# A decode attention block rewritten as one hand-synchronised section

## The chip, the cores and the metric

The kernel runs on one core of one Trainium2 chip. The metric is device time in microseconds, the median of several executions. A core has TensorE (PE in the profile; its weight loads are PEld), VectorE (DVE), ScalarE (ACT), GpSimd (POOL) and SyncE (SP, which here only issues DMAs), and 16 DMA engines that move data between HBM and the on-chip memory (SBUF). TensorE writes its products to a second on-chip memory, PSUM.

## The reference

One decode step of a transformer block: attention over cached keys and values, a feed-forward layer beside it, and a residual sum. All data is float32.

```python
B, Sq, D = 4, 1, 512
H, Sk, Dh = 32, 4096, 128          # k_cache, v_cache: (B, H, Sk, Dh), 268 MB each
F = 1792
xn = _layernorm(x)
q = (xn @ wq).reshape(B, Sq, H, Dh).transpose(0, 2, 1, 3)
scores = einsum("bhqd,bhkd->bhqk", q, k_cache) * Dh ** -0.5
o = einsum("bhqk,bhkd->bhqd", softmax(scores), v_cache)
a = o.transpose(0, 2, 1, 3).reshape(B, Sq, H * Dh) @ wo
f = silu(xn @ w1) @ w2
return x + a + f
```

There is one query row for each batch and head, so every key and every value is used once: 537 MB of caches are read for little arithmetic.

## The kernel before

The work is cut into T = 32 tiles. Tile i is one batch (`i % 4`) and a group of four heads (`i // 4`): 128 partitions, each with R = 128 consecutive positions of 128 numbers, 64 KB a partition, so that 32 partitions hold one head. A tile of K is 8.39 MB and so is a tile of V.

`load_tile` (L72) issues each tile as one DMA from SP. K has two buffers (`kpool`) and V one (`vpool`). The second K buffer first serves as scratch for x, w1 and the intermediate rows, the V buffer first holds wq. A scheduler (the Tile framework) puts in all waits and keeps each engine's instructions in an order of its choice. SP issues in a fixed order: K of tile i+1, then V of tile i.

- `scores` (L228): in four steps of 32 rows, VectorE multiplies K in place by the tile's query, which lies in PSUM spread over the partitions (L235). Of the 32 row sums VectorE takes 24 (`tensor_reduce`, L239); ScalarE takes 8, one `activation` with an accumulated sum each (L241).
- `queries` (L215): once per four tiles, TensorE spreads the queries into PSUM by products with columns of the identity (L221).
- `maxima` and `softmax` (L245, L252): VectorE takes each partition's maximum (L247), TensorE turns the column into a row (L249), VectorE takes the maximum of each head (L255), TensorE spreads it (L259), ScalarE forms the bias (L261) and the four exponentials with their sums (L265). The exponentials go into `p_t`, four columns a row, of which one is not zero.
- `values` (L271): 32 products of TensorE with the V tile, written out in Python for every tile, into one of two PSUM buffers (L277).
- `heads_out` (L285): TensorE sums the exponentials (L289), ScalarE copies the PSUM buffer (L291), VectorE forms the reciprocal and weights (L295, L297), TensorE collects the heads (L300), ScalarE copies them (L305).
- `project` (L307): once per four tiles, the product with a 1 MB piece of wo (`load_wo`, L82, 2 KB runs), added to `acc` in PSUM (L135).

After the last tile, w2 is loaded in four pieces into the V buffer and its products are added to `acc`; VectorE copies it (L359) and four DMAs, two from SP and two from ACT, write the result (L362).

Of the kernel before, what the change touches and what calls it, by code (L numbers as in the profile page):

```python
# [8 lines left out]
F32 = mybir.dt.float32  # L9
# [4 lines left out]
EPS = 1e-5  # L14
G = 4
STEP = 32
ACT_ROWS = 8
LAST_K_CUTS = (64,)
LAST_V_CUTS = (64, 96)
W2_CUTS = (7, 11, 13)  # L20


@with_exitstack
def kernel(
# [11 lines left out]

# [17 lines left out]
    FC = F // P  # L54
    PH = P // G
    R = S * G // P
    T = H // G * B
    NR = 4
# [8 lines left out]
    small = ctx.enter_context(tc.tile_pool(name="small", bufs=2))  # L67
    ps_q = ctx.enter_context(tc.tile_pool(name="ps_q", bufs=2, space=bass.MemoryType.PSUM))
    ps_s = ctx.enter_context(tc.tile_pool(name="ps_s", bufs=3, space=bass.MemoryType.PSUM))
    ps_1 = ctx.enter_context(tc.tile_pool(name="ps_1", bufs=1, space=bass.MemoryType.PSUM))  # L70

    def load_tile(pool, name, cache, i, cuts=()):  # L72
        t = pool.tile([P, R, Dh], F32, name=name)
        h, b = i // B * G, i % B
        src = cache[b, h : h + G].rearrange("h s d -> (h s) d")
        src = src.rearrange("(p r) d -> p r d", p=P)
        edges = (0, *cuts, R)
        for a, z in zip(edges[:-1], edges[1:]):
            nc.sync.dma_start(t[:, a:z, :], src[:, a:z, :])
        return t  # L80

    def load_wo(g):  # L82
        t = wpool.tile([P, G, D], F32, name="wo_t")
        nc.sync.dma_start(
            t, wo[g * G * Dh : (g + 1) * G * Dh, :].rearrange("(h p) n -> p h n", p=P)
        )
        return t


    scratch = kpool.tile([P, R, Dh], F32, name="k_t").rearrange("p r d -> p (r d)")  # L90
    x_sb, xc, sq, xn = (scratch[:B, n * D : (n + 1) * D] for n in range(4))
    NP = 2 * PH - B
    FJ = F // 4
    xpad = scratch[:, 4 * D : 4 * D + DC * NP].rearrange("p (c n) -> p c n", c=DC)
    h_sb = scratch[:, 5 * D : 5 * D + FJ]
    w1_t = scratch[:, 6 * D : 6 * D + DC * F].rearrange("p (c f) -> p c f", c=DC)
    nc.sync.dma_start(x_sb, xf)
    nc.sync.dma_start(w1_t, w1.rearrange("(p c) f -> p c f", p=P))
    wq_t = vpool.tile([P, R, Dh], F32, name="v_t").rearrange("p (c m) d -> p c (m d)", c=DC)
    nc.sync.dma_start(wq_t, wq.rearrange("(p c) n -> p c n", p=P))  # L100
    ks = {0: load_tile(kpool, "k_t", k_cache, 0)}

    ident = const.tile([P, P], F32, name="ident")
    make_identity(nc, ident)
    same = const.tile([P, P], F32, name="same")
    nc.gpsimd.memset(same, 0.0)
    for g in range(G):
        nc.gpsimd.memset(
            same[g * PH : (g + 1) * PH, :].rearrange("p (a g) -> p a g", g=G)[:, :, g], 1.0
        )  # L110
    one = const.tile([1, 1], F32, name="one")
    nc.gpsimd.memset(one, 1.0)
    nc.vector.memset(xpad, 0.0)
    p_t = const.tile([P, R, G], F32, name="p_t")
    nc.gpsimd.memset(p_t, 0.0)

    o_ps = []
    for n in range(2):
        t = ps_1.tile([P, NR * Dh], F32, name=f"o_ps{n}")
        nc.vector.memset(t, 0.0)  # L120
        o_ps.append(t)
    acc = ps_1.tile([P, P], F32, name="acc")
    nc.vector.memset(acc, 0.0)

    pick = const.tile([P, NR * G], F32, name="pick")
    nc.vector.tensor_reduce(
        pick,
        ident.rearrange("p (j m) -> p m j", j=4)[:, : NR * G, :],
        axis=AX, op=ALU.add,
    )  # L130

    def accumulate(lhsT, rhs, start=False, stop=False):

        for j in range(D // P):
            nc.tensor.matmul(  # L135
                acc[32 * j : 32 * j + B, :], lhsT, rhs[:, j * P : (j + 1) * P],
                start=start, stop=stop,
            )

    accumulate(ident[:B, :B], x_sb, start=True)  # L140


    nmean = const.tile([B, 1], F32, name="nmean")
    nc.vector.tensor_reduce(nmean, x_sb, axis=AX, op=ALU.add)
    nc.vector.tensor_scalar_mul(nmean, nmean, -1.0 / D)
    nc.vector.tensor_scalar_add(xc, x_sb, nmean)
    var = const.tile([B, 1], F32, name="var")
    nc.vector.tensor_mul(sq, xc, xc)
    nc.vector.tensor_reduce(var, sq, axis=AX, op=ALU.add)
    nc.vector.tensor_scalar(var, var, 1.0 / D, EPS, op0=ALU.mult, op1=ALU.add)  # L150
    rstd = const.tile([B, 1], F32, name="rstd")
    nc.scalar.activation(rstd, var, AF.Sqrt)
    nc.vector.reciprocal(rstd, rstd)

    t1 = const.tile([B, 1], F32, name="t1")
    nc.vector.tensor_mul(t1, rstd, rstd)
    nc.vector.tensor_mul(t1, t1, var)
    nc.vector.tensor_scalar(t1, t1, -0.5, 1.5, op0=ALU.mult, op1=ALU.add)
    nc.vector.tensor_mul(rstd, rstd, t1)
    nc.vector.tensor_scalar_mul(xn, xc, rstd)  # L160


    xt_ps = ps_s.tile([P, DC, B], F32, name="sm")
    xn_c = xn.rearrange("b (p c) -> b c p", c=DC)
    for c in range(DC):
        nc.tensor.transpose(xt_ps[:, c, :], xn_c[:, c, :], ident[:B, :B])
    xnT = const.tile([P, DC, B], F32, name="xnT")
    nc.vector.tensor_copy(xnT, xt_ps)
    nc.vector.tensor_copy(xpad[:, :, PH - B : PH], xt_ps)

    hp = ps_s.tile([P, FJ], F32, name="sm")
    for c in range(DC):
        for j in range(4):
            nc.tensor.matmul(
                hp[32 * j : 32 * j + B, :], xnT[:, c, :], w1_t[:, c, j * FJ : (j + 1) * FJ],
                start=(c == 0), stop=(c == DC - 1),
            )
    for j in range(4):  # L180
        rows = slice(32 * j, 32 * j + B)
        nc.scalar.activation(h_sb[rows, :], hp[rows, :], AF.Silu)
    ht_ps = ps_s.tile([P, FC, B], F32, name="sm")
    h_f = h_sb.rearrange("b (m f) -> b f m", f=FC)
    for f in range(FC):
        for j in range(4):
            rows = slice(32 * j, 32 * j + B)
            nc.tensor.matmul(
                ht_ps[32 * j : 32 * j + 32, f, :], h_f[rows, f, :], ident[rows, rows],
                start=True, stop=True,  # L190
            )
    hT = const.tile([P, FC, B], F32, name="hT")
    nc.vector.tensor_copy(hT, ht_ps)


    HJ = H // 4
    qp = ps_s.tile([P, Dh], F32, name="sm")
    for hl in range(HJ):
        for c in range(DC):
            for j in range(4):  # L200
                h = HJ * j + hl
                a = PH - B - B * hl
                nc.tensor.matmul(  # L203
                    qp[32 * j : 32 * j + 32, :],
                    xpad[:, c, a : a + PH],
                    wq_t[:, c, h * Dh : (h + 1) * Dh],
                    start=(hl == 0 and c == 0),
                    stop=(hl == HJ - 1 and c == DC - 1),
                )
    q_all = const.tile([P, Dh], F32, name="q_all")  # L210
    nc.vector.tensor_copy(q_all, qp)  # L211

    q_ps, vs, st, ls, ot_g, wo_t = {}, {}, {}, {}, {}, {}

    def queries(n):  # L215

        t = ps_q.tile([P, B, Dh], F32, name="q_ps")
        for b in range(B):
            for g in range(G):
                r = (n * G + g) * B + b  # L220
                nc.tensor.matmul(  # L221
                    t[g * PH : (g + 1) * PH, b, :],
                    ident[:, r : r + 1].to_broadcast([P, PH]), q_all,
                    start=True, stop=True,
                )
            q_ps[n * B + b] = t[:, b, :]

    def scores(i, a):  # L228

        k, q = ks[i], q_ps[i]  # L230
        if a == 0:
            st[i] = small.tile([P, R], F32, name="s")
        s = st[i]
        z = a + STEP
        nc.vector.tensor_tensor(  # L235
            k[:, a:z, :], k[:, a:z, :], q[:, None, :].to_broadcast([P, STEP, Dh]), op=ALU.mult
        )
        v = z - ACT_ROWS
        nc.vector.tensor_reduce(s[:, a:v], k[:, a:v, :], axis=AX, op=ALU.add)  # L239
        for r in range(v, z):  # L240
            nc.scalar.activation(  # L241
                k[:, r, :], k[:, r, :], AF.Copy, accum_out=s[:, r : r + 1]
            )
# [151 lines left out]
```

## Time and profile before

| | |
|---|---|
| runs (3) | 1321.89, 1322.12 and 1322.5 us; median 1322.12 |
| span of the profiled execution, first to last instruction | 1320.8 us |
| busy: VectorE, ScalarE, TensorE, GpSimd | 1008.8, 415.9, 405.6, 1.9 us |
| read from HBM | 561.00 MB, 425 GB/s over the span |

The profile shows one execution. Its span leaves out what lies before the first and after the last instruction, so a run's time is a little longer: 1.3 us at the median. In a group's row stand the line, engine and operation, the tile written and the tile read, the shapes and the count; behind the first bar the busy time in us and the mean of one in ns; behind the second the idle time in front of it and who ended it. In a row in order of time the first two numbers are start and duration in us.

### The profile page before, as it was taken

The page shows a single profiled execution, that of the slowest core. Times are in us where ns is not written, and L with a number is a line of the kernel's source. Part 1 is how long each engine was busy: PE and PEld are TensorE (multiplying, and loading weights), DVE is VectorE, ACT ScalarE, POOL GpSimd, SP SyncE. Part 2 cuts the span into 40 slices and gives each one's busy share as a digit, 9 for nine tenths or more (in the row PEclk, how much of TensorE's full clock was granted, in tenths as well). Part 3 has the DMA queues.
Part 4 walks back from the last instruction along what each step waited for, and adds up shares of the span by engine and source line. Part 5 has one row for each costly group of instructions (what it writes and reads, how often), then busy time and mean ns, then how long its engine had stood idle before and what let it go on. Part 6 is the DMA issues. An engine that isn't in the chain of part 4 may idle for free.

```text
span 1320.8 us, 10238 instructions
## 1 busy us (share of the span) xinstructions
PE 405.6 (31%) x3500; PEld 165.4 (13%) x3500; DVE 1008.8 (76%) x406; ACT 415.9 (31%) x2408; POOL 1.9 (0%) x13
## 2 busy tenths in 40 slices
PE   2312333320343312433322333221334211333207
PEld 1301111100111100111100111010111000111003
DVE  1499967987677986777977777977768977778990
ACT  1143333333333332333232333332323333323331
POOL 0000000000000000000000000000000000000000
PEclk8756666655666656666556666556666556666558
DMA  9999999999999999999999999999999999999996
GB/s 404 436 439 425 429 435 425 439 435 423 441 431 429 427 433 425 439 433 420 442 423 433 437 420 427 433 425 439 422 429 427 431 441 425 431 423 427 425 429 250
DMA packets 14827, 561.65 MB, mean 425 GB/s; under 512 B 1316, under 2 KB 1332, under 8 KB 5688
## 3 DMA queue, kind: packets, MB, share of 16 engines
q1 hardware_dynamic: 14760, 561.01, 98.9%
q8 instruction: 27, 0.44, 0.1%
q14 instruction: 24, 0.20, 0.0%
q10 hardware_dynamic: 16, 0.00, 0.0%
HBM read 561.00 MB, written 0.01 MB: 425 GB/s over the span
## 4 chain that ended last, share of the span: by engine, by line
DMA 54%; DVE 31%; PE 12%; another core or an unknown queue 1%; issue 1%; ACT 0%; SPq 0%; DVEq 0%; ACTq 0%
DMA k_t<-in_A_k_cache_dram 38%; DVE k_t L235 19%; DMA v_t<-in_A_v_cache_dram 13%; DVE s L239 12%; PE o_ps L277 9%; DMA v_t<-in_A_wq_dram 2%; PE q_ps L221 1%; PE sm L203 1%; PE acc L135 0%; ACT o_sb L291 0%; PE sm L300 0%; ACT p_t L265 0%; PE sm L249 0%; DVE m L247 0%
## 5 line engine op out<-in xcount | busy, mean ns | idle before, releaser
L235 DVE TENSOR_TENSOR k_t<-k_t,q_ps 128x4096 f32<-128x4096 f32 x128 | 559.9, 4415 | 204.9 <-DMA k_t<-in_A_k_cache_dram 204.9
L241 ACT ACTIVATE k_t<-k_t 128x128 f32<-128x128 f32 x1024 | 301.4, 295 | 636.3 <-DVE k_t L235 627.8
L277 PE MATMUL o_ps<-v_t,p_t 128*16 128x512 f32 x1984 | 280.9, 729 | 559.9 <-DMA v_t<-in_A_v_cache_dram 556.1
L239 DVE TENSOR_REDUCE s<-k_t 128x24 f32<-128x3072 f32 x128 | 422.9, 3344 | 0.0
L241 ACT ACTIVATION_READ_ACCUMULATOR k_t<-k_t 128x1 f32 x1024 | 191.2, 187 | 0.0
L277 PEld LDWEIGHTS o_ps<-v_t,p_t 128*16 128x16 f32 x1984 | 65.8, 113 | 752.8 <-issue 752.4
L265 ACT ACTIVATE p_t<-s,nb 32x128 f32<-32x128 f32 x128 | 66.0, 516 | 2.5
L221 PE MATMUL q_ps<-q_all,ident 128*32 128x128 f32 x256 | 13.8, 389 | 171.0 <-DVE k_t L235 170.6
L291 ACT ACTIVATE o_sb<-o_ps 128x512 f32<-128x512 f32 x32 | 19.1, 596 | 130.1 <-PE o_ps L277 130.1
L300 PE MATMUL sm<-w,o_sb 128*128 128x4 f32 x256 | 41.5, 285 | 21.9 <-DVE w L297 20.5
L249 PE MATMUL sm<-ident,m 128*1 128x128 f32 x32 | 9.1, 284 | 126.3 <-DVE m L247 126.3
L300 PEld LDWEIGHTS sm<-w,o_sb 128*128 128x128 f32 x256 | 39.6, 236 | 25.4 <-issue 16.9
L305 ACT ACTIVATE ot_g<-sm 128x4 f32<-128x4 f32 x32 | 5.7, 178 | 102.3 <-PE sm L300 102.3
L255 DVE TENSOR_REDUCE gm<-sm 1x4 f32<-1x128 f32 x32 | 8.9, 278 | 30.7 <-PE sm L249 30.7
L221 PEld LDWEIGHTS q_ps<-q_all,ident 128*32 128x32 f32 x256 | 10.2, 156 | 172.6 <-DVE k_t L235 171.1
L265 ACT ACTIVATION_READ_ACCUMULATOR p_t<-s,nb 32x1 f32 x128 | 25.0, 196 | 0.0
L249 PEld LDWEIGHTS sm<-ident,m 128*1 128x1 f32 x32 | 2.5, 79 | 153.8 <-DVE m L247 137.2
L211 DVE COPY q_all<-sm 128x128 f32<-128x128 f32 x1 | 0.3, 292 | 24.0 <-PE sm L203 24.0
L259 PE MATMUL sm<-gm,one 1*128 1x4 f32 x64 | 15.4, 309 | 3.3 <-DVE gm L255 3.3
L295 DVE RECIPROCAL rl<-sm 128x1 f32<-128x1 f32 x32 | 4.8, 150 | 14.5 <-PE sm L289 14.5
L203 PE MATMUL sm<-v_t,k_t 128*32 128x128 f32 x256 | 10.4, 335 | 13.7 <-DMA v_t<-in_A_wq_dram 11.3
L135 PE MATMUL acc<-wo_t,ot_g 128*4 128x128 f32 x256 | 13.6, 380 | 0.3 <-ACT ot_g L305 0.3
(55 smaller groups left out, 117.7 us busy)
## 6 DMA issues: line engine op xcount, KB each, us to landing
wo_t<-in_A_wo_dram SPq DMA_DIRECT2D x8, 1024.0 KB, 49.6
k_t<-in_A_k_cache_dram SPq DMA_DIRECT2D x2, 4096.0 KB, 37.9
k_t<-in_A_v_cache_dram SPq DMA_DIRECT2D x1, 4096.0 KB
k_t<-in_A_v_cache_dram SPq DMA_DIRECT2D x2, 2048.0 KB
k_t<-in_B_w_dram SPq DMA_DIRECT2D x1, 3584.0 KB, 11.3
v_t<-in_B_w_dram SPq DMA_DIRECT2D x1, 1792.0 KB, 13.1
v_t<-in_B_w_dram SPq DMA_DIRECT2D x1, 1024.0 KB, 15.2
v_t<-in_B_w_dram SPq DMA_DIRECT2D x1, 512.0 KB
```

Source lines behind the costliest of these rows:

```text
L135: nc.tensor.matmul(acc[32 * j : 32 * j + B, :], lhsT, rhs[:, j * P : (j + 1) * P], start=start, stop=stop,)
L203: nc.tensor.matmul(qp[32 * j : 32 * j + 32, :], xpad[:, c, a : a + PH], wq_t[:, c, h * Dh : (h + 1) * Dh], start=(hl == 0 and c == 0), sto ...
L221: nc.tensor.matmul(t[g * PH : (g + 1) * PH, b, :], ident[:, r : r + 1].to_broadcast([P, PH]), q_all, start=True, stop=True,)
L235: nc.vector.tensor_tensor(k[:, a:z, :], k[:, a:z, :], q[:, None, :].to_broadcast([P, STEP, Dh]), op=ALU.mult)
L239: nc.vector.tensor_reduce(s[:, a:v], k[:, a:v, :], axis=AX, op=ALU.add)
L241: nc.scalar.activation(k[:, r, :], k[:, r, :], AF.Copy, accum_out=s[:, r : r + 1])
L249: nc.tensor.transpose(mt, m, ident)
L259: nc.tensor.matmul(mb, one.to_broadcast([1, P]), gm, start=True, stop=True)
L265: nc.scalar.activation(p_t[rows, :, g], s[rows, :], AF.Exp, bias=nb[rows, g : g + 1], scale=scale, accum_out=l[rows, :],)
L277: nc.tensor.matmul(o[j : j + NR * G, :], p_t[:, rows, :].rearrange("p r g -> p (r g)"), v[:, rows, :].rearrange("p r d -> p (r d)"), start ...
L291: nc.scalar.activation(o_sb.rearrange("p r d -> p (r d)"), o_ps[i % 2], AF.Copy)
L300: nc.tensor.matmul(ot, o_sb[:, r, :], w[:, r, :], start=(r == 0), stop=(r == NR - 1))
```

## The change

The Tile scheduler's part is replaced by one `tile_critical` section in which every wait is written by hand. A small class, `Queue`, keeps a semaphore and a count for each engine; loads have semaphores of their own.

- Row sums: ScalarE has none left. VectorE multiplies 32 rows as before; GpSimd then adds the upper 64 of a row's 128 products to the lower 64; VectorE sums the 64 that remain (`add`), one step behind.
- Queries: `q_col` holds them as columns. `spread` makes each tile's query in PSUM by one 32 x 32 block transpose of VectorE, in the middle of the tile ahead. The factor -scale is folded into the query, so maxima become minima.
- Maxima: VectorE alone, as a minimum, a transpose and a minimum. The exponential takes the result as its bias directly, and puts its sums into one column of `sums` a tile.
- Values: a hardware loop on TensorE (`Fori`), one body for 31 tiles: wait for the weights and V, 32 products into one PSUM buffer, wait for ScalarE's copy, four collecting products into column i of `o_t`.
- Division by the sums and the product with wo happen once, after all tiles. wo is one load in two pieces (32 KB runs) into the V buffer; w2 goes into a K buffer; the last V goes into the other.
- Placement: small tiles come first, and a fill tile puts the three large buffers on multiples of 256 B. x is loaded from the ACT queue; the output leaves in two DMAs.

The core of the diff (the layer norm and the input products keep their arithmetic):

```diff
-    kpool = ctx.enter_context(tc.tile_pool(name="kpool", bufs=2))
-    vpool = ctx.enter_context(tc.tile_pool(name="vpool", bufs=1))
-    wpool = ctx.enter_context(tc.tile_pool(name="wpool", bufs=1))
+    small([P, -(CONST_AT + taken) % 256 // 4 + 64], "fill")
+    kb = [big.tile([P, R, Dh], F32, name=f"k{n}") for n in range(2)]
+    vb = big.tile([P, R, Dh], F32, name="v")
...
+        got_w1 = load(sp, "w1", w1_t, w1.rearrange("(p c) f -> p c f", p=P))
+        got_x = load(act, "x", x_sb, xf)
+        got_wq = load(sp, "wq", wq_t, wq.rearrange("(p c) n -> p c n", p=P))
+        got_k = {0: load(sp, "k0", kb[0], cache(k_cache, 0))}
...
+        got_k[1] = load(sp, "k1", kb[1], cache(k_cache, 1), p_h, d_h, p_xt)
+        def spread(i):
+            dve.wait(d_col)
+            return dve.done(
+                nc.vector.transpose(
+                    q_b[:, i % 2, :], q_col[:, i, :, None].to_broadcast([P, G, PH])
+                )
+            )
...
+        for i in range(T):
+            k, s = kb[i % 2], s_t[i % 2]
+            if i > 0:
+                if i + 1 < T:
+                    got_k[i + 1] = load(
+                        sp, f"k{(i + 1) % 2}", kb[(i + 1) % 2], cache(k_cache, i + 1),
+                        scored[i - 1],
+                    )
+            if i + 1 < T:
+                got_v[i] = load(
+                    sp, "v", vb, cache(v_cache, i), p_q if i == 0 else (values_done, i)
+                )
+            dve.wait(spread_q[i], got_k[i])
...
+            def add(n):
+                a, z = cuts[n]
+                dve.wait(halves[n])
+                if n == 0 and i > 1:
+                    dve.wait((values_done, i - 1))
+                return dve.done(
+                    nc.vector.tensor_reduce(
+                        s[:, a:z], k[:, a:z, : Dh // 2], axis=AX, op=ALU.add
+                    )
+                )
+            for n, (a, z) in enumerate(cuts):
+                t = dve.done(
+                    nc.vector.tensor_tensor(
+                        k[:, a:z, :], k[:, a:z, :],
+                        q_b[:, i % 2, None, :].to_broadcast([P, z - a, Dh]), op=ALU.mult,
+                    )
+                )
+                pool.wait(t)
+                halves.append(
+                    pool.done(
+                        nc.gpsimd.tensor_tensor(
+                            k[:, a:z, : Dh // 2], k[:, a:z, : Dh // 2], k[:, a:z, Dh // 2 :],
+                            op=ALU.add,
+                        )
+                    )
+                )
+                if n:
+                    add(n - 1)
+            if i + 1 < T:
+                spread_q[i + 1] = spread(i + 1)
+            t = add(len(cuts) - 1)
...
+            t = dve.done(nc.vector.tensor_reduce(m_t, s, axis=AX, op=ALU.min))
...
+            t = dve.done(nc.vector.transpose(mt, m_t.to_broadcast([P, PH])))
...
+            scored[i] = dve.done(nc.vector.tensor_reduce(gm[i % 2], mt, axis=AX, op=ALU.min))
+            if i > 0:
+                act.wait((values_done, i))
+                nc.scalar.activation(
+                    o_sb.rearrange("p r d -> p (r d)"), o_ps, AF.Copy
+                ).then_inc(rows_ready, 1)
+            act.wait(c_zero, scored[i])
+            for g in range(G):
+                rows = slice(g * PH, (g + 1) * PH)
+                t = nc.scalar.activation(
+                    p_t[rows, :, g], s[rows, :], AF.Exp, bias=gm[i % 2][rows, :], scale=-1.0,
+                    accum_out=sums[rows, i : i + 1],
+                )
+            t.then_inc(weights_ready, 1)
+        v_last = kb[(T - 2) % 2]
+        load(sp, "v_last", v_last, cache(v_cache, T - 1), scored[T - 2])
...
+                load(sp, f"wo{n}", wo_t[:, a:z], wo_p[:, a:z], (values_done, T - 1))
...
+            got_w2.append(load(sp, f"w2{n}", w2_t[:, a:z], w2_p[:, a:z], scored[T - 1]))
...
+        with nc.tensor.Fori(0, T - 1) as i:
+            nc.tensor.wait_ge(weights_ready, 1).then_inc(weights_ready, -1)
+            nc.tensor.wait_ge(landed["v"], 16).then_inc(landed["v"], -16)
+            values(vb)
+            collect(o_t[:, bass.ts(i, 1), :].rearrange("p i g -> p (i g)"))
...
+        for n, (a, z) in enumerate(zip(edges[:-1], edges[1:])):
+            pe.wait(got_wo[n])
+            for r in range(a, z):
+                accumulate(xo[:, r, :], wo_t[:, r, :])
...
+        for n, (a, z) in enumerate(zip(f_edges[:-1], f_edges[1:])):
+            pe.wait(got_w2[n])
+            for f in range(a, z):
+                t = accumulate(hT[:, f, :B], w2_t[:, f, :], stop=(f == FC - 1))
...
+        for n in range(2):
+            d_out = nc.vector.tensor_copy(res[0][:, n * P : (n + 1) * P], acc[32 * n : 32 * n + B, :])
+            a_out = nc.scalar.activation(
+                res[1][:, n * P : (n + 1) * P], acc[32 * (n + 2) : 32 * (n + 2) + B, :], AF.Copy
+            )
```

More of the change, by code (lines that the diff above doesn't have):

```diff
@@ L95 @@
[L95 to L109, printed above, removed]
-        )
[L111 to L137, printed above, removed]
-            )
@@ L152 @@
[L152 to L197, printed above, removed]
@@ L198, with small @@
-    for hl in range(HJ):
+    big = ctx.enter_context(tc.tile_pool(name="big", bufs=1))
+    psum = ctx.enter_context(tc.tile_pool(name="psum", bufs=1, space=bass.MemoryType.PSUM))
+    taken = 0
+    def small(shape, name):
+        nonlocal taken
+        taken += -(-4 * math.prod(shape[1:]) // 32) * 32
+        return const.tile(shape, F32, name=name)
+    ident = small([P, P], "ident")
+    p_t = small([P, R, G], "p_t")
+    o_sb = small([P, NR, Dh], "o_sb")
+    s_t = [small([P, R], f"s{n}") for n in range(2)]
@@ new lines @@
+    xpad = small([P, DC, NP], "xpad")
+    hT = small([P, FC, PH], "hT")
+    q_all = small([P, Dh], "q_all")
+    q_col = small([P, T, G], "q_col")
+    xo = small([P, PH, B], "xo")
+    sums = small([P, T], "sums")
+    m_t = small([P, 1], "m")
+    mt = small([P, PH], "mt")
+    gm = [small([P, 1], f"gm{n}") for n in range(2)]
+    pick = small([P, NR * G], "pick")
+    quad = small([P, G, 4], "quad")
+    perm = small([P, P], "perm")
+    ones = small([P, 1], "ones")
+    rl = small([P, B], "rl")
@@ L358 @@
-    res = small.tile([P, P], F32, name="s")
-    nc.vector.tensor_copy(res, acc)
-    for j in range(D // P):
-        eng = nc.sync if j % 2 == 0 else nc.scalar
-        eng.dma_start(of[:, j * P : (j + 1) * P], res[32 * j : 32 * j + B, :])
+                t = nc.tensor.matmul(
+                    ps_a[32 * j : 32 * j + 32, :], xpad[:, c, PH - B : 2 * PH - B],
+                    w1_t[:, c, j * FJ : (j + 1) * FJ], start=(c == 0), stop=(c == DC - 1),
+                )
+        p_h = pe.done(t)
@@ new lines @@
+        p_q = pe.done(t)
+        dve.wait(p_q)
+        d_q = dve.done(nc.vector.tensor_scalar_mul(q_all, ps_q, -scale))
+        pe.wait(d_q)
+        heads = ident.rearrange("p (n g b) -> p g n b", g=G, b=B)
+        for g in range(G):
+            for a in range(4):
+                t = nc.tensor.matmul(
+                    ps_b[32 * g : 32 * g + 32, 32 * a : 32 * a + 32],
+                    q_all[:, 32 * a : 32 * a + 32], heads[:, g], start=True, stop=True,
+                )
+        p_col = pe.done(t)
@@ new lines, with values @@
+        for n, (a, z) in enumerate(zip(f_edges[:-1], f_edges[1:])):
+            got_w2.append(load(sp, f"w2{n}", w2_t[:, a:z], w2_p[:, a:z], scored[T - 1]))
+        act.wait((values_done, T))
+        nc.scalar.activation(
+            o_sb.rearrange("p r d -> p (r d)"), o_ps, AF.Copy
+        ).then_inc(rows_ready, 1)
+        def values(v):
+            n = R // NR
+            for m in range(n):
+                j = 32 * (m % 4)
+                rows = slice(m * NR, (m + 1) * NR)
+                t = nc.tensor.matmul(
+                    o_ps[j : j + NR * G, :],
+                    p_t[:, rows, :].rearrange("p r g -> p (r g)"),
+                    v[:, rows, :].rearrange("p r d -> p (r d)"),
+                    start=(m < 4), stop=(m >= n - 4),
+                )
+            t.then_inc(values_done, 1)
```

400 lines of the change are left out of this document (229 added, 171 removed).

## The prediction

> **What bounds the kernel now.** I read the page first: busy shares, the slices, the DMA queues.
>
> ```profile
> span 1320.8 us, 10238 instructions
> PE 405.6 (31%) x3500; PEld 165.4 (13%) x3500; DVE 1008.8 (76%) x406; ACT 415.9 (31%) x2408; POOL 1.9 (0%) x13
> PEclk8756666655666656666556666556666556666558
> DMA  9999999999999999999999999999999999999996
> q1 hardware_dynamic: 14760, 561.01, 98.9%
> q8 instruction: 27, 0.44, 0.1%
> q14 instruction: 24, 0.20, 0.0%
> ```
>
> No engine is full; the DMA is, in every slice but the last. So the groups should show compute waiting for loads, and the times of those waits give the pace:
>
> ```profile
> L235 DVE TENSOR_TENSOR k_t<-k_t,q_ps 128x4096 f32<-128x4096 f32 x128 | 559.9, 4415 | 204.9 <-DMA k_t<-in_A_k_cache_dram 204.9
> L277 PE MATMUL o_ps<-v_t,p_t 128*16 128x512 f32 x1984 | 280.9, 729 | 559.9 <-DMA v_t<-in_A_v_cache_dram 556.1
> L239 DVE TENSOR_REDUCE s<-k_t 128x24 f32<-128x3072 f32 x128 | 422.9, 3344 | 0.0
> 191.26 8.75 DVE L235 TENSOR_TENSOR k_t<-k_t,q_ps 128x4096 f32<-128x4096 f32 x2 [7.71 <-DMA k_t<-in_A_k_cache_dram]
> 229.82 4.42 DVE L235 TENSOR_TENSOR k_t<-k_t,q_ps 128x4096 f32<-128x4096 f32 x1 [6.73 <-DMA k_t<-in_A_k_cache_dram]
> 269.19 8.75 DVE L235 TENSOR_TENSOR k_t<-k_t,q_ps 128x4096 f32<-128x4096 f32 x2 [7.53 <-DMA k_t<-in_A_k_cache_dram]
> 307.98 8.75 DVE L235 TENSOR_TENSOR k_t<-k_t,q_ps 128x4096 f32<-128x4096 f32 x2 [6.96 <-DMA k_t<-in_A_k_cache_dram]
> 350.00 8.75 DVE L235 TENSOR_TENSOR k_t<-k_t,q_ps 128x4096 f32<-128x4096 f32 x2 [6.81 <-DMA k_t<-in_A_k_cache_dram]
> ```
>
> Each row in time is the landing of a K tile. The steps are 38.56, 39.37, 38.79 and, with a `wo_t` load inside, 42.02 us. K and V of one tile are 2 x 128 x 64 KB = 16.78 MB, so the fast steps (mean 38.68) are 434 GB/s. At that pace all 561.0 MB take 561.0/16.78 x 38.68 = 1293.4 us. The real stream is longer; its two ends, in windows of 2 us whose last columns are the DMA's share and GB/s:
>
> ```profile
> 0.00:2.00 2.00, 0.00 (x0) 0.00 (x0) 0.98 (x3) 1.27 (x1) 1.33 (x11) 1.00 0.02 4
> 2.00:4.00 2.00, 0.60 (x8) 0.13 (x8) 1.90 (x6) 0.01 (x1) 0.60 (x3) 1.00 1.14 358
> 1306.00:1308.00 2.00, 2.00 (x24) 0.48 (x20) 0.00 (x0) 0.00 (x0) 0.00 (x0) 0.92 0.90 363
> 1308.00:1310.00 2.00, 2.00 (x24) 0.46 (x20) 0.00 (x0) 0.00 (x0) 0.00 (x0) 1.00 0.19 76
> 1312.00:1314.00 2.00, 1.58 (x28) 1.49 (x32) 0.00 (x0) 0.28 (x2) 0.00 (x0) 1.00 0.06 26
> L349 SPq DMA_DIRECT2D v_t<-in_B_w_dram x4: 327/431/534, 1297.2 to 1298.5; - x4
> v_t<-in_B_w_dram SPq DMA_DIRECT2D x1, 256.0 KB, 16.2
> 1314.35 3.24 PE L135 MATMUL acc<-v_t,hT 128*4 128x128 f32 x112
> 1317.65 0.29 DVE L359 COPY s<-acc 128x128 f32<-128x128 f32 x1 [14.61 <-PE acc L135]
> ```
>
> A share of 0.06 is one of 16 DMA engines. Fifteen finish near 1308; one goes on, and the last piece of w2, issued at 1298.5, lands 16.2 us later at 1314.7. The stream starts at 2.0; a stream at the fast pace would end at 1295.4. So the last engine carries 1314.7 - 1295.4 = **19.3 us of extra**, and a tile is usable only when the last engine has landed.
>
> What is the extra? The page has two queues of instruction fetches. The 7000 PE and PEld entries times 63 B are q8's 0.44 MB; ACT, DVE and POOL, 2827 entries, would at 71 B be q14's 0.20 MB, in 24 packets of 8 KB. A slow step less a fast one (39.37 less 38.68) is 0.7 us, and 24 x 0.7 = 16.8. My reading, which the rows support but do not prove: q14's packets go through one of the 16 engines and hold its K and V rows up by 0.7 us each. The step with `wo_t` is 42.02 against 38.68 + 2.42 (1.05 MB at 434 GB/s) + 0.7 = 41.80, so 0.2 us too long; `wo_t` is the load cut into 2 KB runs: 8 x 0.2 = 1.6. That leaves 0.9 of the 19.3.
>
> **The change, part by part. Fetches.** The row sums leave ACT: 2 x 1024 entries go, and ACT keeps 8 entries of exponentials and an eviction for each of 32 tiles, some 300. DVE has 12 a tile, 383 in all; POOL gains 4 a tile, 138 in all. 821 of 2827 is 0.29: 24 packets become 7, 16.8 us become **4.9**. PE's stored program shrinks by about four times, as one loop body stands for 31 tiles. **wo.** 8.39 MB once, in 32 KB runs, on SP behind the last V and ahead of w2: the same bytes, less **1.6**. I take the remaining 0.9 as it is. The stream then ends at 1295.4 + 4.9 + 0.9 = **1301.2**.
>
> **Placement.** The fill tile moves K and V to multiples of 256 B; before, they start 128 B past one. No row prices that. I bound it by the spread of the fast steps, 38.56 to 38.79: 0.3% or 4 us either way, and take zero, as both ends occur with the buffers of before. [...]
>
> **The tail.** Now the w2 products (112 passes, 3.24 us) end 2.9 us after the last landing, and the span ends 3.2 us after that (1317.6 to 1320.8: copy and output DMA). After, w2 is taken in four pieces as they land and the last piece is 8 passes, 0.3 us. Output has two copies of 4 rows on each of two engines where it was one of 128, and one DMA a queue where it was two: taken as even, between -0.5 and +0.5. The span ends at 1301.2 + 0.3 + 3.2 = **1304.7**. Everything else at the end hides under wo and w2, 12.06 MB or 27.8 us behind the last V: its values (8.8 us below), eviction, transposes and small products (some 3 us), and wo's 256 passes at 3.24/112 us (7.4). Cover gone, they cost about 20 us. The granted clock falls to half between stages (PEclk), and passes at half clock take twice as long; I allow 2 us.
>
> **What must stay hidden: the loads.** SP keeps the order K, V, K, V; a wait there holds every later load.
>
> ```profile
> 210.57 8.76 PE L277 MATMUL o_ps<-v_t,p_t 128*16 128x512 f32 x64 [25.54 <-DMA v_t<-in_A_v_cache_dram]
> 219.39 0.33 SPq L79 DMA_DIRECT2D v_t<-in_A_v_cache_dram  x1
> 221.78 0.33 SPq L79 DMA_DIRECT2D k_t<-in_A_k_cache_dram  x1
> 2.13 0.52 POOL L115 MEMSET p_t<- 128x512 f32 x1
> 1.11 0.29 POOL masks.py:199 TENSOR_SCALAR_AFFINE_SELECT ident<-ident 128x128 f32<-128x128 f32 x1
> L247 DVE TENSOR_REDUCE m<-s 128x1 f32<-128x128 f32 x32 | 9.2, 286 | 3.2
> 46.36 0.44 SPq L79 DMA_DIRECT2D v_t<-in_A_v_cache_dram  x1
> 52.39 8.75 DVE L235 TENSOR_TENSOR k_t<-k_t,q_ps 128x4096 f32<-128x4096 f32 x2 [6.14 <-DMA k_t<-in_A_k_cache_dram]
> ```
>
> The V landing at 210.57 is multiplied by 219.3, V's buffer is reissued at 219.39, and K occupies the DMA until 229.82: 10.4 us ahead of need. The loop keeps that: same 64 passes, one V buffer. It adds two waits in front of each tile's values (weights, V) and one before the collecting products; behind them only PE's own next tile is queued. Back edge and register address are not in the trace: between nothing and PE's 25.54 us of idle before a tile, they cost nothing, since a tile's products are followed by that idle.
>
> **VectorE and GpSimd, per tile.** Four multiplies (4.415) and four reduces of 2048 elements where they were 3072 (3.344 x 2/3 = 2.23) are 26.6 us; a query transpose, a minimum, a transpose and a minimum, 0.3 each as L247, make 27.8. Before, multiplies and reduces alone were 31.0. GpSimd's add, 2048 outputs, is not in the trace. Below, four 512-element memsets: 2.1 us. Above, sixteen 128-element selects: 4.6. I take the upper, nearest in kind (it reads). Then VectorE waits a little for GpSimd in the first and last quarter and the tile's scores are ready 30.1 us after landing, against a step of 38.7: 8.6 us free. SP's wait for the K buffer now includes the minima (0.9 us), inside that. The bound breaks only when an add passes (38.7 - 4.4 - 2.2 - 0.9)/4 = 7.8 us. [...]
>
> **Start.** K1 no longer waits for the query product, since the scratch lies elsewhere, and V0 still does; before, both went out by 46.4 and K0 was used only at 52.39, so the DMA always had work. The third K needs tile 0's scores: 52.4 + 30.1 = 82.5, against two loads behind K0, 52.4 + 38.7 = 91.1. No gain; a first add that is up to 8 us slow costs nothing.
>
> **Sum.** 1304.7 span; the runs' median, 1322.12, is 1.3 above the span, so **1306.0 us**, 16.1 or 1.2% faster. The bounds: 4.9 less if the remaining fetches fall ahead of the stream, 4 either way for placement, 0.5 either way for output, 2 more for the clock: 1296.6 to 1312.5.
>
> **Rivals.** *The late engine stays late* (0.2): it is slow for another reason than ACT's fetches. For it: a packet's engine is in no view. Then only wo (1.6) and the tail (2.6) come off: 1317.9; with half the fetch gain, 1312. *GpSimd and VectorE exclude each other* (0.07): 27.8 + 4 x 4.6 = 46.2 us a tile, 7.5 above the step, 32 x 7.5 = 240 us slower, about 1546; it decides as soon as an add holds VectorE for over (38.7 - 27.8)/4 = 2.7 us. [...] *The loop fetches its body anew* (0.08): 31 x 16 KB, twice an 8 KB packet, 1.4 us each if one DMA engine serves them: 43 us on that engine, 1349; spread over all, 3 us. More than 12 on one engine (16.1/1.4) make the kernel slower. Against it: q8's 27 packets before cost no engine as much as q14's. [...] *Gain and some loss cancel* (0.05): within 0.2%, which is about what can be told from no change here (2.6 us).
>
> **How the numbers follow.** The forecast has 0.6, the late engine 0.2, the two slower rivals 0.15, cancelling 0.05. Faster 0.8, same 0.05, slower 0.15. The range takes the forecast's own bounds and the late engine: 1297 to 1318.
>
> **What would show it.** Right: last DMA window full to within 2 us of the last landing, near 1301; K steps of 38.7 without the 39.4 kind; q14 at about 7 packets; GpSimd adds of 4 to 5 us; VectorE idle 8 us a tile on K. Wrong: VectorE multiplies above 4.5 us or K steps set by VectorE; q8 above 27 packets; idle DMA between V and K; one DMA engine still alone for 6 us at the end.

## The result, and the profile after

The changed kernel takes 1304.14 us (median of 4 runs, 1303.93 to 1304.39), the kernel before, on the same chip, 1322.31 (4 runs, 1321.89 to 1322.54). The ratio is 0.9866, with a 95% interval of 0.9852 to 0.988: 18.2 us or 1.3% faster. The forecast was 1306.0 with a range of 1297 to 1318. On other chips below, the kernel before took 1320.7 to 1321.6; each experiment is set against the runs beside it.

The page of the changed kernel, some of the parts shown of before, and its first two groups:

```profile
span 1302.2 us, 7259 instructions
PE 361.1 (28%) x3014; PEld 124.1 (10%) x3014; DVE 882.4 (68%) x411; ACT 90.4 (7%) x295; POOL 580.0 (45%) x136
...
DMA  9999999999999999999999999999999999999998
...
q1 hardware_dynamic: 10376, 561.00, 99.5%
q8 instruction: 6, 0.10, 0.0%
q14 instruction: 8, 0.07, 0.0%
```

```profile
L338 POOL TENSOR_TENSOR k<-k 128x2048 f32<-128x2048 f32 x128 | 578.8, 4533 | 677.1 <-DVE k L330 677.1
L330 DVE TENSOR_TENSOR k<-k,q_b 128x4096 f32<-128x4096 f32 x128 | 562.3, 4413 | 257.5 <-DMA k<-in_A_k_cache_dram 257.5
```

The bytes are the same and the DMA is still the only thing that is full, now to the end: q1's share rose from 98.9 to 99.5%. Both queues of instruction fetches shrank, q14 from 24 packets to 8 and q8 from 27 to 6. ScalarE fell from 416 us to 90, GpSimd rose from 2 to 580.

In order of time (start, duration), one tile and then landings of K:

```profile
187.27 8.75 DVE L330 TENSOR_TENSOR k<-k,q_b 128x4096 f32<-128x4096 f32 x2 [8.65 <-DMA k<-in_A_k_cache_dram]
...
206.67 9.63 PE L396 MATMUL o_ps<-v,p_t 128*16 128x512 f32 x64 [28.13 <-PEq L416]
...
214.14 2.29 DVE L323 TENSOR_REDUCE s<-k 128x32 f32<-128x2048 f32 x1 [2.24 <-POOL k L338]
...
216.35 0.33 SPq L156 DMA_DIRECT2D v<-in_A_v_cache_dram  x1
...
217.03 0.19 DVE L354 TENSOR_REDUCE gm<-mt 128x1 f32<-128x32 f32 x1
217.24 0.33 SPq L156 DMA_DIRECT2D k<-in_A_k_cache_dram  x1
...
264.51 8.75 DVE L330 TENSOR_TENSOR k<-k,q_b 128x4096 f32<-128x4096 f32 x2 [8.72 <-DMA k<-in_A_k_cache_dram]
303.19 8.75 DVE L330 TENSOR_TENSOR k<-k,q_b 128x4096 f32<-128x4096 f32 x2 [8.72 <-DMA k<-in_A_k_cache_dram]
...
882.76 8.75 DVE L330 TENSOR_TENSOR k<-k,q_b 128x4096 f32<-128x4096 f32 x2 [8.68 <-DMA k<-in_A_k_cache_dram]
922.22 8.75 DVE L330 TENSOR_TENSOR k<-k,q_b 128x4096 f32<-128x4096 f32 x2 [9.53 <-DMA k<-in_A_k_cache_dram]
960.82 8.75 DVE L330 TENSOR_TENSOR k<-k,q_b 128x4096 f32<-128x4096 f32 x2 [8.65 <-DMA k<-in_A_k_cache_dram]
```

The scores of the tile that landed at 187.27 are complete at 217.22, 29.95 us later, and VectorE then waits over 8 us for the next K: loads set the pace. The steps are 38.6 us, and one is 39.46 (882.76 to 922.22); in the kernel before, from 191.26 to 1224.44, 12 of the 20 steps without a piece of `wo` were of this long kind. From 187.27 to 960.82 are 20 steps, 38.68 on average with that one in it.

The end, first in windows (duration, five engines, granted clock, DMA share, GB/s), then the last links of the chain:

```profile
1294.00:1296.00 2.00, 2.00 (x74) 1.85 (x77) 0.00 (x0) 0.00 (x0) 0.00 (x0) 1.00 0.83 330
1296.00:1298.00 2.00, 1.80 (x59) 1.14 (x56) 0.00 (x0) 0.00 (x0) 0.00 (x0) 1.00 0.15 57
1298.00:1300.00 2.00, 0.22 (x8) 0.00 (x0) 0.56 (x2) 0.54 (x2) 0.00 (x0) 1.00 0.01 4
```

```profile
1262.38 34.76 DMA k<-in_B_w_dram
1297.14 0.04 issue
1297.18 0.62 PE acc L226 x16
1297.81 0.02 issue
1297.82 0.45 PE acc L226 x8
1298.27 0.03 issue
1298.29 0.28 DVE k L480
1298.57 0.01 issue
1298.58 0.28 DVE k L480
```

The last piece of w2 lands at 1297.14, within 2 us of the last full window; before, one DMA engine ran on alone for some 6 us and the last landing was at 1314.7. So of the 18.6 us that the span lost, 17.6 lie in the stream of loads and 1 in what follows it (5.1 us where it was 6.1).

### The profile page after: what moved, and what is told of

It reads as the page before. It is cut to its first block, busy times and chain, and to the rows that moved or that the text cites. A ratio compares the mean times of both kernels' runs of the same rounds, so it can differ in the third digit from the quotient of the medians.

```text
span 1302.2 us, 7259 instructions
## 1 busy us (share of the span) xinstructions
PE 361.1 (28%) x3014; PEld 124.1 (10%) x3014; DVE 882.4 (68%) x411; ACT 90.4 (7%) x295; POOL 580.0 (45%) x136
## 3 DMA queue, kind: packets, MB, share of 16 engines
q1 hardware_dynamic: 10376, 561.00, 99.5%
## 5 line engine op out<-in xcount | busy, mean ns | idle before, releaser
L338 POOL TENSOR_TENSOR k<-k 128x2048 f32<-128x2048 f32 x128 | 578.8, 4533 | 677.1 <-DVE k L330 677.1
L330 DVE TENSOR_TENSOR k<-k,q_b 128x4096 f32<-128x4096 f32 x128 | 562.3, 4413 | 257.5 <-DMA k<-in_A_k_cache_dram 257.5
L396 PE MATMUL o_ps<-v,p_t 128*16 128x512 f32 x1984 | 285.8, 740 | 869.3 <-PEq L416 869.3
L323 DVE TENSOR_REDUCE s<-k 128x32 f32<-128x2048 f32 x128 | 292.1, 2282 | 81.8 <-POOL k L338 81.8
L396 PEld LDWEIGHTS o_ps<-v,p_t 128*16 128x16 f32 x1984 | 67.2, 113 | 1062.1 <-issue 1062.1
L364 ACT ACTIVATE p_t<-s,gm 32x128 f32<-32x128 f32 x128 | 66.0, 515 | 34.5 <-DVE gm L354 32.6
L407 PE MATMUL o_t<-pick,o_sb 128*128 128x4 f32 x256 | 33.6, 254 | 30.6 <-PEq L405 30.6
L407 PEld LDWEIGHTS o_t<-pick,o_sb 128*128 128x128 f32 x256 | 31.0, 191 | 59.9 <-issue 59.9
L364 ACT ACTIVATION_READ_ACCUMULATOR p_t<-s,gm 32x1 f32 x128 | 25.0, 195 | 0.0
L261 PE MATMUL ps_q<-v,xpad 128*32 128x128 f32 x256 | 10.1, 328 | 15.5 <-DMA v<-in_A_wq_dram 13.5
L427 DVE TENSOR_TENSOR k<-sums,quad 128x512 f32<-128x512 f32 x1 | 0.7, 692 | 17.6 <-PE o_ps L396 17.6
L261 PEld LDWEIGHTS ps_q<-v,xpad 128*32 128x32 f32 x256 | 9.2, 134 | 17.1 <-DMA v<-in_A_wq_dram 14.6
```

Source lines behind the costliest of these rows:

```text
L261: t = nc.tensor.matmul(ps_q[32 * j : 32 * j + 32, :], xpad[:, c, a : a + PH], wq_t[:, c, h * Dh : (h + 1) * Dh], start=(hl == 0 and c == 0 ...
L323: nc.vector.tensor_reduce(s[:, a:z], k[:, a:z, : Dh // 2], axis=AX, op=ALU.add)
L330: nc.vector.tensor_tensor(k[:, a:z, :], k[:, a:z, :], q_b[:, i % 2, None, :].to_broadcast([P, z - a, Dh]), op=ALU.mult,)
L338: nc.gpsimd.tensor_tensor(k[:, a:z, : Dh // 2], k[:, a:z, : Dh // 2], k[:, a:z, Dh // 2 :], op=ALU.add,)
L364: t = nc.scalar.activation(p_t[rows, :, g], s[rows, :], AF.Exp, bias=gm[i % 2][rows, :], scale=-1.0, accum_out=sums[rows, i : i + 1],)
L396: t = nc.tensor.matmul(o_ps[j : j + NR * G, :], p_t[:, rows, :].rearrange("p r g -> p (r g)"), v[:, rows, :].rearrange("p r d -> p (r d)") ...
```

## The experiments

**Is it the fetches?** The theory: ScalarE's stored instructions are fetched by q14 over the same DMA engines, and each packet delays the engine that ends last. Rivals: the work on ScalarE itself, or another cause for the late engine. Three kernels give ScalarE or GpSimd of the changed kernel idle work of their own, which nothing waits for (the lines shown leave out the tiles and waits of that work).

`e1_act_pad`: 32 small sums on ScalarE for each tile.

```
+ for r in range(PH):
+     t = nc.scalar.activation(pad_out[:, 4*r : 4*r+4], pad_in[:, 4*r : 4*r+4], AF.Copy,
+                              accum_out=pad_sum[:, r : r+1])
```

> The changed kernel with 32 more ScalarE instructions a tile behind the exponentials (128x4 copies with an accumulated sum, on tiles of their own; 2 trace entries each, 2048 in all, as many as the change took out), in ScalarE's idle time and waited for by nobody. Fetch theory (non-PE instruction fetches hold up one DMA engine by 0.7 us each): 2048 entries by 71 B are 18 more 8 KB packets on q14, the last engine ends 12.4 us later, 1304.1 becomes 1316.5. Rival (the gain came from row sums leaving ScalarE's and VectorE's timing, or from loads issued in time): 1304, as no other engine waits for these instructions.

`e2_act_loop`: the same sums as a loop of ScalarE, stored once a tile instead of 32 times.

```
+ with nc.scalar.Fori(0, PH - 1) as r:
+     nc.scalar.activation(pad_out[:, bass.ts(r, 4)], pad_in[:, bass.ts(r, 4)], AF.Copy,
+                          accum_out=pad_sum[:, bass.ts(r, 1)])
```

> The same 32 ScalarE instructions a tile, 31 of them as a hardware loop of one instruction: as many are executed, only about six a tile are stored. Fetch theory: q14 grows by about 2 packets, 1304 to 1306. Rival (ScalarE's execution itself, its reads and writes in SBUF, slows the loads): as e1_act_pad, 1316. If a loop's back edge fetched anew, q14 would be far above 24 packets and the time above 1316.

`e8_pool_pad`: 64 memsets of one element for each tile on GpSimd, as many stored entries as the 32 sums make.

```
+ for r in range(64):
+     nc.gpsimd.memset(pad_out[:, 2*r : 2*r+1], 0.0)
```

> The changed kernel with 64 more GpSimd instructions a tile (memsets of one column in a tile of their own, about 0.1 us each, behind the last add; 2048 in all); GpSimd has 20 us idle a tile. Fetch theory if all engines but TensorE share the late DMA engine: 16 to 18 more q14 packets, 1316. If each engine's fetches have a DMA engine of their own: the same number of packets and again about 12 us on another engine, also 1316, the time cannot tell these two apart. If only ScalarE's fetches cost: 1304.

On one chip, against 1321.49 for the kernel before: written out on ScalarE 1314.02 (ratio 0.9935, 0.9919 to 0.9952), looped 1304.15 (0.9869, 0.9852 to 0.9885), written out on GpSimd 1312.27 (0.9925, 0.9909 to 0.9942). From the page of the first, then from its windows:

```profile
q14 instruction: 24, 0.20, 0.0%
...
L376 ACT ACTIVATE pad_out<-pad_in 128x4 f32<-128x4 f32 x1024 | 194.4, 191 | 0.9
```

```profile
1302.00:1304.00 2.00, 2.00 (x84) 1.78 (x76) 0.00 (x0) 0.00 (x0) 0.00 (x0) 1.00 0.14 56
1304.00:1306.00 2.00, 1.88 (x72) 1.40 (x60) 0.00 (x0) 0.00 (x0) 0.00 (x0) 1.00 0.10 37
1306.00:1308.00 2.00, 1.21 (x40) 0.91 (x44) 0.00 (x0) 0.00 (x0) 0.00 (x0) 1.00 0.06 24
```

and from the page of the looped one:

```profile
PE 360.5 (28%) x3014; PEld 124.0 (10%) x3014; DVE 882.5 (68%) x411; ACT 381.1 (29%) x2343; POOL 579.8 (45%) x137
...
q14 instruction: 9, 0.07, 0.0%
```

and from the page and groups of the one on GpSimd:

```profile
q14 instruction: 24, 0.20, 0.0%
...
L351 POOL MEMSET pad_out<- 128x1 f32 x2048 | 69.7, 100 | 0.0
```

The loop keeps ScalarE busier (381.1 us) than the written-out sums do and costs nothing; the written-out sums bring q14 back to 24 packets, the 9.9 us and the picture of the end: one or two DMA engines alone (shares 0.14, 0.10, 0.06) for 6 us after the others. So it is the stored entries that cost, not ScalarE's work, and they cost on GpSimd too. Against the looped kernel, whose q14 has 9 packets, there are 15 more: on average a packet costs 9.9/15 = 0.66 us of the whole time for ScalarE's entries and (1312.27 - 1304.15)/15 = 0.54 for GpSimd's, where the prediction had 0.7.

The kept trace also holds the start of every packet, and in the kernel before this ties the long steps to q14: each of the 12 long ones (39.31 us or more) among the 20 steps without a piece of `wo` has a packet of q14 in it, and none of the 8 short ones (38.82 or less) has. q8's packets lie in both kinds. A step with two packets of q14 (508.89 to 548.26, 39.37 us) is no longer than one with a single packet, so not each of them costs.

**The other way, in the kernel before.** `e4_act_rows12`: more row sums on ScalarE.

```
- ACT_ROWS = 8
+ ACT_ROWS = 12
```

> The kernel before with 12 of every 32 row sums on ScalarE instead of 8 (ACT_ROWS 8 to 12): 512 more sums, each two entries on its queue, so 1024 more entries; VectorE has less to do. Fetch theory, at the price that 1024 padding pairs showed in the changed kernel (9.9 us for 16 packets of 8 KB, 0.62 each): about 8 to 9 packets more, 5 to 6 us slower, ratio 1.004, and a last slice of the page with less in it. Rival (what delays the last engine has nothing to do with ScalarE's queue): no change, or a little faster because VectorE has more slack, ratio 1.000 or below.

1327.29 us against 1321.62 (ratio 1.0041, 1.0027 to 1.0054): 5.7 us slower with 8 packets more, 0.71 each. From its page, then from its order of time:

```profile
q14 instruction: 32, 0.26, 0.0%
```

```profile
390.93 8.75 DVE L235 TENSOR_TENSOR k_t<-k_t,q_ps 128x4096 f32<-128x4096 f32 x2 [9.83 <-DMA k_t<-in_A_k_cache_dram]
...
430.30 8.75 DVE L235 TENSOR_TENSOR k_t<-k_t,q_ps 128x4096 f32<-128x4096 f32 x2 [9.55 <-DMA k_t<-in_A_k_cache_dram]
...
469.69 8.75 DVE L235 TENSOR_TENSOR k_t<-k_t,q_ps 128x4096 f32<-128x4096 f32 x2 [9.70 <-DMA k_t<-in_A_k_cache_dram]
```

Now nearly every step is of the slow kind (39.37 and 39.39), as there is about one packet a tile. VectorE had less to do and waited longer for each K (9.7 us where it was 7), which did not help.

`e3_act_rows0`: no row sums on ScalarE, all 32 on VectorE, GpSimd not used.

```
- ACT_ROWS = 8
+ ACT_ROWS = 0
```

> The kernel before with one number changed: ScalarE sums none of the rows, VectorE all 32 (ACT_ROWS 8 to 0); GpSimd stays idle, the values stay unrolled, wo stays in eight pieces. 2048 entries fewer. Fetch theory: q14 24 to 6 packets, 12.4 us less, 1322.3 becomes 1310; VectorE has 4 x (4.415 + 4.46) + 0.9 = 36.4 us a tile, under the step of 38.7. Rival (late engine for another reason, or late issue of V): 1322. Third: VectorE becomes the bound through its stops between tiles: above 1322.

The theory's 1310 failed, and the third case that the expectation named came: 1332.76 us, ratio 1.0076 (1.0059 to 1.0093), slower than before, though q14 fell to 7 packets. In turn from its groups, from SP's waits (total, times, longest), from its windows and from its order of time:

```profile
L239 DVE TENSOR_REDUCE s<-k_t 128x32 f32<-128x4096 f32 x128 | 559.4, 4412 | 0.0
```

```profile
SPq L79 <- DVE m L247: 156.4, 24, 17.2
```

```profile
190.00:200.00 10.00, 8.24 (x75) 4.10 (x67) 8.38 (x7) 2.03 (x8) 0.00 (x0) 0.96 0.43 152
```

```profile
1226.06 8.75 DVE L235 TENSOR_TENSOR k_t<-k_t,q_ps 128x4096 f32<-128x4096 f32 x2 [2.53 <-DMA k_t<-in_A_k_cache_dram]
...
1296.88 0.29 DVE L247 TENSOR_REDUCE m<-s 128x1 f32<-128x128 f32 x1
```

and from the order of time of the kernel before:

```profile
1286.74 0.29 DVE L247 TENSOR_REDUCE m<-s 128x1 f32<-128x128 f32 x1
```

Four multiplies and four full reduces are 4 x (4.415 + 4.412) = 35.3 us of VectorE a tile, with 2.53 us to spare in a step of 38.7. SP now waits for VectorE's maxima 24 times, 156 us in all; in the kernel before it waited for VectorE's sums 22 times, 75 us in all. Where the start puts VectorE behind, the DMA idles (a share of 0.43 in the window from 190). At the end the last scores are 10 us later than before (1296.88 to 1286.74), and w2, whose buffer the last values must free first, is loaded later with them. The expectation had taken 36.4 us of VectorE as enough under a step of 38.7. Between the ends it is: the K that landed at 229.82 in the kernel before lands at 237.60, 7.8 us late, and the one of 1224.44 at 1226.06, 1.6 late. At the start and the end, where loads wait for VectorE, 2.5 us of slack are too few. The fetches did go (most steps without a piece of wo are 38.7), but here the sums left ScalarE with profit only where GpSimd took a share of them.

**What else is in the gain.** Four kernels on one chip, with the kernel before at 1320.73 us. `after_again` is the changed kernel; the others undo one thing each.

> The changed kernel once more, as the yardstick of the three runs beside it, on the same chip. All theories: 1304.1 us, within 0.5; K steps of 38.63 us.

It took 1304.65 us (1304.21 to 1306.2; ratio 0.9879, 0.9862 to 0.9895).

`e5_values_unrolled`:

```
- with nc.tensor.Fori(0, T - 1) as i:
+ for i in range(T - 1):
...
-     collect(o_t[:, bass.ts(i, 1), :].rearrange("p i g -> p (i g)"))
+     collect(o_t[:, i, :])
```

> The changed kernel with the values of tiles 0 to 30 written out instead of looped, so TensorE's stored program grows back by about 31 x 64 products with their weight loads. Theory (a fetch costs what it holds up on the one engine that ends last): q8 goes from 6 packets to about 26 of 16 KB; if they are spread over the 16 engines the last engine gets one or two, so 1304 to 1306 us. Rival 1 (every fetched byte costs the same, wherever it goes: ScalarE's padding cost 9.9 us for 16 packets of 8 KB): 20 packets of 16 KB cost 20 to 25 us, so 1324 to 1329. Rival 2 (the loop itself costs something, by its back edge or its register addresses): unrolled is faster than 1304.

1307.05 us (1306.13 to 1307.81; ratio 0.9892, 0.9876 to 0.9909), with

```profile
q8 instruction: 23, 0.38, 0.1%
```

on its page, 17 packets more: 2.4 us, or 0.14 us for a packet of 16 KB where q14's of 8 KB cost 0.5 to 0.7. So here the price of a fetch did not go by its bytes; TensorE's cost less. The value lies just above the theory's 0 to 2 and far from the 20 of the first rival. The two ratios' intervals overlap; the runs themselves do not, but for one of the changed kernel.

`e6_off128`:

```
- small([P, -(CONST_AT + taken) % 256 // 4 + 64], "fill")
+ small([P, -(CONST_AT + taken) % 256 // 4 + 96], "fill")
```

> The changed kernel with the fill tile 128 bytes longer, so that the K and V buffers start 128 B past a multiple of 256 B in each partition, as before the change. If placement costs nothing: 1304.1 us and K steps of 38.63. [...]

1306.97 us (1306.91 to 1307.21; ratio 0.9895, 0.9878 to 0.9911), 2.3 us slower. Two landings of K, twelve steps apart, first with the 128 B offset:

```profile
148.91 8.75 DVE L330 TENSOR_TENSOR k<-k,q_b 128x4096 f32<-128x4096 f32 x2 [7.13 <-DMA k<-in_A_k_cache_dram]
...
613.38 8.75 DVE L330 TENSOR_TENSOR k<-k,q_b 128x4096 f32<-128x4096 f32 x2 [8.76 <-DMA k<-in_A_k_cache_dram]
```

and in `after_again`:

```profile
148.74 8.75 DVE L330 TENSOR_TENSOR k<-k,q_b 128x4096 f32<-128x4096 f32 x2 [6.91 <-DMA k<-in_A_k_cache_dram]
...
612.35 8.75 DVE L330 TENSOR_TENSOR k<-k,q_b 128x4096 f32<-128x4096 f32 x2 [8.67 <-DMA k<-in_A_k_cache_dram]
```

The steps are 464.47/12 = 38.706 and 463.61/12 = 38.634 us: 0.072 us, or 0.19%, in each, and 561.0/16.78 = 33.4 steps make 2.4 us, the whole difference. So placement does cost here; why it does is not shown.

`e7_wo_short`:

```
- wo_p = wo.rearrange("(p r) n -> p r n", p=P)
+ wo_p = wo.rearrange("(r p) n -> p r n", p=P)
```

> The changed kernel with wo loaded in runs of 2 KB (row r x 128 + p on partition p, where it was row p x 16 + r in runs of 32 KB); the rows of wo then meet other rows of the collected values, so the output product is of the wrong pairs, at the same work. The prediction's term (0.2 us for each MB of 2 KB runs, 8 MB): 1.6 us more, 1305.7. Rival (the 0.2 was only the spread of steps): 1304.1.

1305.21 us (1305.12 to 1305.4; ratio 0.9881, 0.9865 to 0.9898): 0.6 us, not to be told from nothing beside the spread of `after_again`, and less than the 1.6 of the prediction.

**Do the parts add up?** `e9_all_back` has the changes of `e1_act_pad`, `e5_values_unrolled` and `e6_off128` at once.

> The changed kernel with three of its savings given back at once, the hand-synchronised order and GpSimd's adds kept: the padding sums on ScalarE (1024 pairs, alone +9.9 us), the values of 31 tiles written out (alone +2.4), the buffers 128 B past a multiple of 256 (alone +2.3). Theory (the gain is a sum of these, all of them time of the DMA engines): 14.6 us over the changed kernel, about 1319, ratio 0.9985 or so, 1 to 2 us short of the kernel before; what is left is wo's short runs (0.6) and the longer end. Rival (the delays overlap, since only the last of 16 engines counts and the fetches of TensorE go to others): about 12 us, the 9.9 and the 2.3, so 1316 to 1317, ratio 0.9965. If the order of the work itself, or the split with GpSimd, had brought most of the gain: 1310 or less.

1316.28 us against 1321.62 (ratio 0.996, 0.9948 to 0.9973). The three alone are 9.9 + 2.4 + 2.3 = 14.6 us; together they cost about 12 (1316.28 less 1304.1 to 1304.7, which are from other chips; by the ratios to the kernel before it is 10.7 to 12.4). That is the figure of the rival, in which TensorE's fetches disappear behind the engine that ends last. Landings of K, 28 steps apart, show which part disappears; first `e1_act_pad`:

```profile
148.77 8.75 DVE L335 TENSOR_TENSOR k<-k,q_b 128x4096 f32<-128x4096 f32 x2 [6.89 <-DMA k<-in_A_k_cache_dram]
...
1241.88 8.75 DVE L335 TENSOR_TENSOR k<-k,q_b 128x4096 f32<-128x4096 f32 x2 [9.52 <-DMA k<-in_A_k_cache_dram]
```

and `e9_all_back`:

```profile
149.16 8.75 DVE L335 TENSOR_TENSOR k<-k,q_b 128x4096 f32<-128x4096 f32 x2 [7.62 <-DMA k<-in_A_k_cache_dram]
...
1243.86 8.75 DVE L335 TENSOR_TENSOR k<-k,q_b 128x4096 f32<-128x4096 f32 x2 [9.55 <-DMA k<-in_A_k_cache_dram]
```

They take 1093.11 and 1094.70 us. The 1.6 more is no more than placement alone adds (28 x 0.072 = 2.0), so nothing is left for TensorE's fetches; alone they made the same 28 steps 2.2 us longer (1084.88 in `e5_values_unrolled`, 1082.63 in `after_again`). Together the three take back some 70% of the gain with the hand-written order, the split with GpSimd and the new end in place.

Two kernels do one part of the change alone in the kernel before. `e10_before_wo_long`:

```
- t, wo[g * G * Dh : (g + 1) * G * Dh, :].rearrange("(h p) n -> p h n", p=P)
+ t, wo[g * G * Dh : (g + 1) * G * Dh, :].rearrange("(p h) n -> p h n", p=P)
```

> The kernel before with each 1 MB piece of wo loaded in runs of 8 KB (row p x 4 + h on partition p, where it was row h x 128 + p in runs of 2 KB); the rows of wo then meet other rows of the values, so the output product is of the wrong pairs, at the same work. The prediction's term: 8 x 0.2 = 1.6 us faster than before, ratio 0.9988, and steps with wo of about 41.8 where they were 42.0. By what the short runs cost at the end of the changed kernel: 0.6 us, ratio 0.9995, not to be told from no change. A gain of 3 us or more would close the gap that is left between the kernel before and the one with three savings given back.

`e11_before_aligned`:

```
+ nc.gpsimd.memset(const.tile([P, 32], F32, name="fill"), 0.0)
  p_t = const.tile([P, R, G], F32, name="p_t")
```

> The kernel before with 128 bytes more in its pool of constants, so that K and V start at multiples of 256 B in each partition (one small memset more on GpSimd at the start). If placement costs here what it costs in the changed kernel (0.07 us a K step, 2.3 in all): 2.3 us faster, ratio 0.9982, K steps near 38.6 and 39.3 where they were 38.7 and 39.4. Rival (the last engine waits on fetches and the others wait for it, so a faster pace is hidden): no change, ratio 1.000.

Against 1321.14: longer runs of wo 1320.08 (ratio 0.9991, 0.9982 to 1.0), 1.1 us with an interval that reaches no change (three steps with a piece of wo and no packet of q14 are 41.18, 41.17 and 41.03 where they were 41.31, 41.39 and 41.24, so 0.19 us a piece and 1.5 for eight); aligned buffers 1317.56 (ratio 0.9969, 0.9959 to 0.9978), 3.6 us faster, between 2.9 and 5.4 by the interval. So placement pays in the kernel before too, and its rival (a faster pace hidden behind the late engine) falls; the 2.3 us expected of it were too few.

Between `e9_all_back` and the kernel before, 5.3 us are left. Some 1.1 are wo's runs, as far as they are real, and 1.0 the longer end. About 3 us stay open: the price of placement is 1.3 larger in the kernel before than in the changed one, and the rest was not told apart.

## Why the prediction was right, and where it was not

**The bound and the pace.** Right: the DMA is full to the end. The pace was put at 38.68 us a tile and is 38.63, which over 33.4 tiles ends the stream 1.7 us earlier. The term mis-sized here is placement: it was taken at zero between ends of -4 and +4, and is -2.3 (`e6_off128`). The spread of single steps could not show it: the fast ones of the forecast lie up to 0.23 us apart (38.56 to 38.79), and placement adds 0.07 to each.

**Fetches.** The forecast stood on a reading that the rows did not prove. That stored entries cost time, and through q14's packets, is shown by `e1_act_pad` against `e2_act_loop`, by the long steps of the kernel before and by the slower `e4_act_rows12`; that one DMA engine bears them stays a reading. The packets left were forecast at 7 and are 8. The price was 0.7 us each and measures 0.5 to 0.7 on average of those added. Those that remain cost less than the 4.9 us put down for them, and not for the reason that the bound named (fetches that fall ahead of the stream): by the kept trace six of the eight start between 117.5 and 887.1 us, inside the stream, and two after the last landing. Five of the six lie in steps behind the landing at 148.66. Only one of these five steps is longer, by 0.8 us (39.46); the other four are 38.60 to 38.65. So the step that gave each packet the same price was too simple; which packets cost nothing, and why, is not shown. Missing from the sum were TensorE's fetches: "q8's 27 packets before cost no engine as much as q14's" is right, yet by itself the loop is worth 2.4 us (`e5_values_unrolled`).

**wo.** Forecast at 1.6 us, from one step that was 0.2 us too long; the times give 0.6 and 1.1, neither clear of zero, and the steps of the kernel before bear the 0.2 out (0.19).

**The stream's end.** Forecast at 1301.2, measured 1297.14: 4.1 us early, 1.7 of it the pace and the rest, by difference, mostly the remaining fetches.

**The end after it.** Forecast at 0.3 + 3.2 = 3.5 us, measured 5.1. The last landing releases 24 passes in place of 8 (the chain's 0.62 and 0.45 us, 1.1 in all), because the last two pieces of w2 became usable almost together; and VectorE makes its two copies one after the other, 0.56 us where the chain of before had 0.29. The rest is from the last copy to the span's end, 3.3 us. This error has the other sign: 4.1 early, 1.6 late, and 0.6 because the median now lies 1.9 us above the span where 1.3 was assumed, make the 1.9 us between 1306.0 and 1304.1. That the total came so close is in part luck. Of the 2 us allowed for the clock nothing shows: 1.00 was granted from 1294 to 1300. (In the kernel before, 2 us of L203 hold 44 passes at 0.50, from 34 to 36, and 83 at 1.00, from 38 to 40.)

**The tile.** GpSimd's add was put between 2.1 and 4.6 us and taken at 4.6: 4.533. Scores after 30.1 us: 29.95. 8.6 us free: 8.65 to 8.72. The multiply next to GpSimd takes 4.413 us, where it took 4.415 with GpSimd idle, so the rival in which the two exclude each other falls. The loop's rival falls with q8 at 6 packets; the late engine's with `e2_act_loop`. Waits in front of the values cost nothing: SP reissues V at 216.35 and K at 217.24, 8.6 us ahead of the K that lands at 225.87.

## What to carry to other kernels

In a kernel that the DMA bounds, count the stored instructions of engines that seem idle: where an engine had many, each packet fetched for it cost 0.5 to 0.7 us here, and a loop over the same work got it back. Move work off an engine for its fetches only after working out the slack of the engine that receives it; with VectorE left 2.5 us to spare, a saving became a loss (`e3_act_rows0`, 1332.76 us against 1321.49). Then align large buffers to 256 B, which was worth 2.3 and 3.6 us here for a few bytes.

## What the runs showed of the hardware that was not expected

A fetch of 8 KB for ScalarE's or GpSimd's entries, where many were added, cost the kernel 0.5 to 0.7 us on average (0.66 in `e1_act_pad`, 0.54 in `e8_pool_pad`, 0.71 in `e4_act_rows12`), about four times what a fetch of 16 KB by TensorE cost (0.14 in `e5_values_unrolled`, from two medians whose intervals overlap). At the stream's 434 GB/s one of 16 engines moves 27.1, which makes 0.30 us of 8 KB, and the kept traces have 0.31 us for most such packets: the price is about twice that. Not every packet has it (four of five in the changed kernel's steps cost nothing: 38.60 to 38.65 us). That one DMA engine at a time bears them is a reading: a share of 0.06, one of 16, is what runs on at the end of `e1_act_pad` (from 1306) and of the kernel before (from 1312). A loop on ScalarE of 32 rounds a tile added no cost that 4 runs can see (1304.15 beside 1304.14), and writing out TensorE's gained nothing (1307.05 beside 1304.65). And with K and V 128 B past a multiple of 256 B, in rows of 64 KB, a K step took 38.706 us where it took 38.634, 0.19% more (`e6_off128`, `after_again`).
